# Layer-norm reciprocal square roots by Ln and Exp on ScalarE, and mixed-V stores on another queue

## The chip, the cores and the metric

The kernel runs on one core of a Trainium2 chip. The metric is the device time of one execution in microseconds (us), as a median over runs; the kernel before takes 297.19 us (three runs, 296.29 to 297.81). Engines are named as in the profile: PE is TensorE, PEld its weight loads, DVE VectorE, ACT ScalarE, POOL GpSimd, SP SyncE. A run is called slow when it lies over 1.5% above the fastest of the same kernel, the other runs fast.

## The reference, cut to what matters

Attention over blocks that a Sinkhorn-normalised matrix has mixed, then a Fourier mix of the result, a layer norm and a feed-forward network. The change is about the line with `sqrt`, and about how `v_sorted` reaches the attention.

```python
k_sorted = einsum('bhij,bhjcd->bhicd', P, k_b)     # P: five Sinkhorn steps on sort_net
v_sorted = einsum('bhij,bhjcd->bhicd', P, v_b)     # the "mixed V"
x   = softmax(scale * q_b @ k_sb.T) @ v_sb         # laid out (4, 768, 512)
u   = x + real(fft(fft(x, axis=1), axis=2))
un  = (u - mean(u)) / sqrt(var(u) + 1e-6)          # over 512 columns
out = u + relu(un @ w_ch1) @ w_ch2                 # 512 -> 2048 -> 512
```

## The kernel before

The kernel first collects all its operations with `P.add(costs, fn, r=reads, w=writes)` and then orders them with a small scheduler of its own. `costs` names the engines that may run the operation, each with (time that it occupies the engine, time to its result). The scheduler, where an operation may run on ACT or DVE, takes the engine that its plan says is free first. The hardware then runs each engine's operations in the planned order.

The layer norm of one group (three tiles of 128 rows; two groups in each of four batches, so eight norms) works on a 128x3 tile of variances, on GpSimd:

```python
P.add({"POOL": (0.25, 0.25)}, lambda _: G.tensor_scalar(
    mv.ap[:, :, 1], mv.ap[:, :, 1], 1e-6, None, op0=ALU.add), ...)
P.add({"POOL": (0.9, 0.9)}, lambda _: G.tensor_tensor(
    ny.ap, mv.ap[:, :, 1], mhalf, op=ALU.pow), ...)          # (var + eps) ** -0.5
P.add({"POOL": (0.2, 0.2)}, lambda _: G.tensor_tensor(
    nm.ap, mv.ap[:, :, 0], ny.ap, op=ALU.mult), ...)
P.add({"POOL": (0.25, 0.25)}, lambda _: G.tensor_scalar(
    nm.ap, nm.ap, -1.0, None, op0=ALU.mult), ...)
...  # then un = u * ny + nm, on ACT or DVE, three tiles
```

The mixed V of a pair of batches is stored to DRAM by SyncE and gathered back into another layout by GpSimd:

```python
for hb in range(2):                 # the pair's two batches
    for k_ in range(3):
        P.add({"SP": (0.4, 4.2)}, lambda _, ...:
              nc.sync.dma_start(vdr[t][w64, cols], vm[w64, cols]), ...)
        o = P.add({"POOL": (1.3, 1.3)}, lambda _, ...:
              nc.gpsimd.dma_start(vsb[...], vdr[t][w64, cols]...), ...)
```

The feed-forward's first matmul fills a PSUM bank with four matmuls; the bank is then emptied with a ReLU (`hr`) by ACT or DVE, as the plan decides. This emptying is called an eviction below.

The softmax here doesn't subtract the row's maximum and nothing guards it: scores larger than these inputs give would overflow.

Of the kernel before, what the change touches and what calls it, by code (L numbers as in the profile page):

```python
# [9 lines left out]
F32 = mybir.dt.float32  # L10
F16 = mybir.dt.float16
AF = mybir.ActivationFunctionType
ALU = mybir.AluOpType
# [8 lines left out]
DM = 512  # L22
# [348 lines left out]
def kernel(  # L371
# [10 lines left out]
    nc = tc.nc  # L382
# [6 lines left out]
    def ct(name, shape, dtype):  # L389
        return const.tile(shape, dtype, name=name)  # L390

    P = Plan()

    def many(name, n, shape, dtype):
        P.pool(name, [ct(f"{name}{i}", shape, dtype) for i in range(n)])
# [39 lines left out]
    many("y", 1, [128, 4, 2 * NK], F16)  # L435
    many("hi", 1, [128, 258], F16)
    many("u", 6, [128, DM], F32)
    many("un", 2, [128, DM], F16)
    many("ut", 2, [128, 4, GT], F16)
    tab = ct("tab", [128, 2, 2, 257], F32)  # L440
    cs = ct("cs", [128, 2, 3, 2 * NK], F16)
# [10 lines left out]
    vbn = ct("vbn", [128, D], F16)  # L452
    rows = ct("rows", [128, 3 * B], mybir.dt.uint32)
    negone = ct("negone", [128, 1], F32)
    mhalf = ct("mhalf", [128, 3], F32)
    mone = ct("mone", [128, 3], F32)
    many("rz", 4, [128, 6], F32)
    many("st", 3, [128, 6], F32)
    many("mv", 2, [128, 3, 2], F32)
# [66 lines left out]
    def hk(g):  # L526
        return [("h", g, fc) for fc in range(16)]

    def load_v(t, hf, prio):
        if t == 0:  # L530
            load(nat[0][:, 3072 * hf:3072 * hf + 3072].rearrange(
                "p (c d) -> p c d", d=D),
                vv[0:128, 48 * hf:48 * hf + 48, :], 1572864,
                [("nat", 0, hf)] + hk(0)[8 * hf:8 * hf + 8], prio)
            return
        keys = kqk(2 * hf) + kqk(2 * hf + 1)
        past = {o for n in keys for d_ in (P.wr, P.rd) for o in d_.get(n, ())}
        for n in keys:
            P.wr[n], P.rd[n] = [], []
        for r in range(3 * hf, 3 * hf + 3):  # L540
            load(nat[1][:, 1024 * r:1024 * r + 1024].rearrange(
                "p (c d) -> p c d", d=D),
                vv[128:256].rearrange(
                    "p (c r) d -> p r c d", r=6)[:, r], 690000,
                [("nat", 1, r)], prio + 0.01 * r, after=tuple(past))
            P.ops[-1].late = 0.0
            for n in keys:
                P.wr[n].append(P.ops[-1])
# [10 lines left out]
    V = nc.vector  # L559
    for n in range(NEB):  # L560
# [3 lines left out]
              tag="ebz")  # L564
    for n in range(2):
# [4 lines left out]
        vsb[0:96, :, D:D + 1], 1.0 / XSC), w=["vsz"], prio=-200.0, tag="vsz")  # L570
    P.add({"POOL": (0.1, 0.4)}, lambda _: nc.gpsimd.memset(
        pmt[:, 4:7, DM:DM + 2], 0.0), w=["pmz"], prio=-150.0, tag="small")
    for t_, val in ((negone, -1.0), (mhalf, -0.5), (mone, 1.0)):
        P.add({"POOL": (0.1, 0.4)}, lambda _, t_=t_, val=val:
              nc.gpsimd.memset(t_, val), w=["smalls"], prio=-199.0, tag="small")
    P.add({"POOL": (0.9, 0.9)}, lambda _: nc.gpsimd.tensor_tensor(
        mone, mone, mhalf, op=ALU.pow), r=["smalls"], w=["mone"], prio=-198.0,
        tag="small")

    early = dict(  # L580
        pw=(pw, sort_net.rearrange("b h i j -> (b h) i j"), 8192),
# [167 lines left out]
    def v_mix(t):  # L749
        bd = bdv16[t].rearrange("p g i -> p (g i)")  # L750
        stage = [i for n in range(4) for i in kqk(n)] if t else hk(0)
        vm = nat[1] if t else hr[1].rearrange("p a b -> p (a b)")
        vmk = [] if t else hk(1)
        n4 = nat[t].rearrange(
            "p (r c d) -> p r c d" if t else "p (c r d) -> p r c d",
            r=6, d=D)
        for n in range(12):
            r, hf = divmod(n, 2)
            ps = Buf("pm", "pf")

            def f(_, r=r, hf=hf, ps=ps):
                o = ps.ap.rearrange("p (c d) -> p c d", d=D)
                nc.tensor.matmul(o, bd, n4[:, r, 8 * hf:8 * hf + 8],
                                 start=True, stop=(t == 1))
                if t == 0:
                    nc.tensor.matmul(
                        o, bd, vbn[:, None, :].broadcast_to([128, 8, D]),
                        start=False, stop=True)
            P.add(pe(mm(512, 2 - t)), f,
                  r=[("nat", t, r if t else hf), ("bdv16", t)] + stage  # L770
                  + (["vbn"] if t == 0 else []), w=[ps], tag="vmix")
            P.add({"ACT": act(512), "DVE": dve(512)},
                  lambda e, n=n, ps=ps: copy(
                      e, vm[:, 512 * n:512 * n + 512], ps.ap),
                  r=[ps] + vmk, w=[("vm", t, n)] + (
                      [("nat", 1, r)] if t else []), tag="vev")
        for hb in range(2):
            w64 = slice(64 * hb, 64 * hb + 64)
            for k_ in range(3):
                cols = slice(2048 * k_, 2048 * k_ + 2048)  # L780
                P.add({"SP": (0.4, 4.2)}, lambda _, w64=w64, cols=cols:
                      nc.sync.dma_start(vdr[t][w64, cols], vm[w64, cols]),
                      r=[("vm", t, n) for n in range(4 * k_, 4 * k_ + 4)]
                      + (stage if t else vmk), w=[("vdr", t, k_, hb)],
                      prio=P.prio + 6 * hb, tag="vst")
                o = P.add({"POOL": (1.3, 1.3)},
                          lambda _, k_=k_, w64=w64, cols=cols:
                          nc.gpsimd.dma_start(  # L788
                              vsb[32 * k_:32 * k_ + 32, w64, 0:D],
                              vdr[t][w64, cols].rearrange(  # L790
                                  "g (c d) -> c g d", d=D)),
                          r=[("vdr", t, k_, hb), "vsz"],
                          w=[("vsb", k_, hb)],
                          prio=P.prio if hb == 0 or t else 38.0,
                          tag="vgt", nbytes=690000)
                gets[t, hb].append(o)
# [390 lines left out]
    def dft2(b, g):  # L1187
# [11 lines left out]
        for tt in range(3):  # L1199
# [62 lines left out]
                mv.ap[:, tt, :], st.ap), r=[st], w=[(mv, tt)], tag="bna")  # L1262
        ny, nm = Buf("ny"), Buf("nm")
        mvs = [(mv, tt) for tt in range(3)]
        G = nc.gpsimd
        P.add({"POOL": (0.25, 0.25)}, lambda _: G.tensor_scalar(  # L1266
            mv.ap[:, :, 1], mv.ap[:, :, 1], 1e-6, None, op0=ALU.add),
            r=mvs, w=[(mv, 3)], tag="ln")
        P.add({"POOL": (0.9, 0.9)}, lambda _: G.tensor_tensor(
            ny.ap, mv.ap[:, :, 1], mhalf, op=ALU.pow),  # L1270
            r=[(mv, 3), "mone"], w=[ny], tag="ln")
        P.add({"POOL": (0.2, 0.2)}, lambda _: G.tensor_tensor(
            nm.ap, mv.ap[:, :, 0], ny.ap, op=ALU.mult),
            r=[(mv, 3), ny], w=[nm], tag="ln")
        P.add({"POOL": (0.25, 0.25)}, lambda _: G.tensor_scalar(
            nm.ap, nm.ap, -1.0, None, op0=ALU.mult), r=[nm], w=[(nm, 1)],
            tag="ln")
        lns.append(P.ops[-1])
        ut = Buf("ut")
        uts[b, g] = ut  # L1280
        for tt in range(3):
            un, pt, u = Buf("un"), Buf("pf"), us[b, g][tt]

            def f(e, tt=tt, un=un, u=u):
                if e == "ACT":
                    nc.scalar.activation(un.ap, u.ap, AF.Identity,  # L1286
                                         scale=ny.ap[:, tt:tt + 1],
                                         bias=nm.ap[:, tt:tt + 1])
                else:
                    V.tensor_scalar(un.ap, u.ap, ny.ap[:, tt:tt + 1],  # L1290
                                    nm.ap[:, tt:tt + 1],
                                    op0=ALU.mult, op1=ALU.add)
            P.add({"ACT": (0.72, 0.81), "DVE": (0.45, 0.55)}, f,
                  r=[u, ny, (nm, 1)], w=[un], tag="un")
            if b > 0:
                P.add({"SP": (1.3, 4.0)}, lambda _, tt=tt, un=un:
                      nc.sync.dma_start_transpose(
                          ut.ap[:, :, 128 * tt:128 * tt + 128], un.ap),
                      r=[un], w=[(ut, tt, 1)], tag="uX")
                continue  # L1300

            def f(_, un=un, pt=pt):
                p16 = pt.ap.bitcast(F16)
                for c in range(4):
                    nc.tensor.matmul(
                        p16[:, 128 * c:128 * c + 128],
                        un.ap[:, 128 * c:128 * c + 128], idh,
                        is_transpose=True)
            P.add(pe(0.27), f, r=[un, "pack"], w=[pt, (ut, tt)], tag="uT")
            P.add({"ACT": act(512), "DVE": dve(512, 2.0)},  # L1310
                  lambda e, tt=tt, pt=pt: copy(
                      e, ut.ap[:, :, 128 * tt:128 * tt + 128],
                      pt.ap.bitcast(F16)[:, 0:512].rearrange(
                          "p (c s) -> p c s", c=4)),
                  r=[pt], w=[(ut, tt, 1)], tag="utev")
# [156 lines left out]
```

## Time and profile before

| profiled run of before | value |
|---|---|
| span | 293.2 us |
| PE busy | 257.1 us (88%) |
| ACT busy | 145.1 us (49%) |
| DVE, POOL busy | 173.9 us, 84.8 us |
| mean granted PE clock (share of the full clock) | 0.963 |
| ACT table loads | 1 |

The forty slices and the stretches say where PE has holes: before 143 us it has some, after that none. The timelines of ACT, DVE and PE say which bank waits for which eviction. A bracket such as `[2.56 <-ACT ex L1030]` at the end of a line means that the engine stood still 2.56 us before this instruction, and that the named write by ACT ended the wait. The lines themselves stand in the prediction.

### The profile page before, as it was taken

To read this page: it belongs to the slowest core of one execution; us is meant where nothing else is said; L and a number is where in the kernel's file an instruction comes from. 1 tells how busy PE (TensorE), PEld (TensorE's weight loads), DVE (VectorE), ACT (ScalarE), POOL (GpSimd) and SP (SyncE) were. 2 spreads that over 40 slices of the span, in tenths; PEclk is the share of its full clock that TensorE was granted. 3 is DMA by queue.
4 is the path that set the end of the run, shared out by engine and by line. 5 is a ranking of instruction groups with operands and counts; after the bars stand their busy time and mean duration, and the time that the engine had idled before them with its cause. 6 is when DMAs were issued, how large, how long until landed. Compare 5 with 4: busy or idle time off the path is not lost.

```text
span 293.2 us, 5526 instructions
## 1 busy us (share of the span) xinstructions
PE 257.1 (88%) x2124; PEld 146.9 (50%) x2124; DVE 173.9 (59%) x407; ACT 145.1 (49%) x307; POOL 84.8 (29%) x120
## 2 busy tenths in 40 slices
PE   0698697769999999696999999999999999999980
PEld 0255484465555464453557456456555545545530
DVE  6899879896999997384999452146124315310020
ACT  2289649666642586643697126327514505605400
POOL 8914843049730056830220001023000212200021
PEclk9999759987999999999999999999999999999997
DMA  7999999999996369999303011411311131141001
GB/s 128 202 203 287 217 229 173 213 209 141 164 173 122 80 162 221 170 144 153 92 22 57 2 72 36 56 72 50 56 72 37 36 56 72 36 92 36 0 36 72
DMA packets 56543, 32.60 MB, mean 111 GB/s; under 512 B 42842, under 2 KB 51560, under 8 KB 56516
## 3 DMA queue, kind: packets, MB, share of 16 engines
q0 software_dynamic: 36592, 21.46, 50.6%
q1 hardware_dynamic: 19926, 10.80, 16.8%
q8 instruction: 16, 0.26, 0.4%
q14 instruction: 9, 0.07, 0.1%
HBM read 32.12 MB, written 9.44 MB: 142 GB/s over the span
## 4 chain that ended last, share of the span: by engine, by line
PE 47%; DMA 3%; issue 1%; DVE 1%; POOLq 0%; DVEq 0%
PE bank L1326 21%; PE bank L1347 20%; DMA out_dram<-u,rows 3%; PE bank L1221 1%; PE bank L1133 1%; PE bank L1060 1%; PE bank L1225 1%; PE bank L1021 1%; POOLq L1467 0%; PE bank L966 0%; PE bank L1138 0%; PE bank L1209 0%; DVE u L1355 0%; DVE u L1245 0%; PE bank L1143 0%
## 5 line engine op out<-in xcount | busy, mean ns | idle before, releaser
L1326 PE MATMUL bank<-ut,w1sb 128*128 128x384 f16 x512 | 93.8, 330 | 3.0 <-DVE u L1355 2.8
L1338 ACT ACTIVATE hr<-bank 128x384 f16<-128x384 f32 x109 | 53.3, 490 | 71.1 <-PE bank L1326 70.4
L1347 PE MATMUL bank<-w2sb,hr 128*128 128x512 f16 x384 | 87.8, 379 | 0.0
L1326 PEld LDWEIGHTS <-w1sb 128*128 128x128 f16 x512 | 48.9, 99 | 38.0 <-issue 5.0
L1347 PEld LDWEIGHTS <-hr 128*128 128x128 f16 x384 | 36.9, 98 | 41.7 <-issue 0.2
L1355 DVE TENSOR_TENSOR u<-bank,u 128x512 f32<-128x512 f32 x24 | 16.5, 690 | 54.5 <-PE bank L1347 54.2
L1030 ACT ACTIVATE ex<-bank 96x384 f32<-96x384 f32 x64 | 28.4, 485 | 10.7 <-PE bank L1021 10.2
L1368 POOL DMA_INDIRECT out_dram<-u,rows x12 | 12.1, 1006 | 72.4 <-DVE u L1355 54.4
L1266 POOL TENSOR_SCALAR mv<-mv 128x3 f32<-128x3 f32 x8 | 1.9, 240 | 78.8 <-DVE mv L1261 75.7
L788 POOL DMA_DIRECT2D vsf<-vdr x12 | 13.0, 1088 | 34.8 <-DMA vdr<-kq 23.4
L1060 PE MATMUL bank<-vsf,eb 97*128 97x65 f16 x416 | 18.6, 206 | 2.6 <-DMA vsf<-vdr 1.6
L1060 PEld LDWEIGHTS <-eb 97*128 97x128 f16 x416 | 16.8, 107 | 5.2 <-issue 2.8
L1045 ACT ACTIVATE eb<-ex,negone 96x384 f16<-96x384 f32 x31 | 18.5, 613 | 0.3
L486 POOL DMA_DIRECT2D kq<-in_q_dram x20 | 16.4, 833 | 6.9 <-DMA kq<-in_k_dram 2.1
L1286 ACT ACTIVATE un<-u,nm,ny 128x512 f16<-128x512 f32 x15 | 12.2, 811 | 11.4 <-DMA ut<-un 9.1
L1076 DVE TENSOR_TENSOR rt<-bank,rz 128x384 f16<-128x384 f32 x32 | 17.2, 549 | 0.4
L1245 DVE SCALAR_TENSOR_TENSOR u<-rt,bank 128x510 f32<-128x510 f16 x12 | 8.1, 679 | 15.5 <-DMA out_dram<-u,rows 9.9
L1233 DVE SCALAR_TENSOR_TENSOR u<-rt,bank 128x512 f32<-128x512 f16 x12 | 8.0, 685 | 14.8 <-PE bank L1225 14.8
L1259 DVE BATCH_NORM_STATS2 st<-u 128x6 f32<-128x512 f32 x24 | 16.1, 682 | 0.2
L1021 PE MATMUL bank<-qt,ks 64*128 64x96 f16 x256 | 12.8, 213 | 3.7 <-ACT ex L1030 2.9
L966 PE MATMUL bank<-bdk,kq 128*64 128x128 f16 x192 | 10.6, 228 | 3.4 <-ACT ex L1030 1.5
L694 ACT CAST ks<-bank 128x384 f16<-128x384 f32 x18 | 8.2, 484 | 10.7 <-PE bank L966 10.6
(137 smaller groups left out, 317.3 us busy)
## 6 DMA issues: line engine op xcount, KB each, us to landing
kq<-in_k_dram POOLq DMA_DIRECT2D x8, 384.0 KB, 10.1
vsf<-vdr POOLq DMA_DIRECT2D x12, 256.0 KB, 6.9
w1sb<-in_moe_w_ch_dram POOLq DMA_DIRECT2D x4, 512.0 KB, 16.9
w2sb<-in_moe_w_ch_dram POOLq DMA_DIRECT2D x4, 512.0 KB, 19.3
out_dram<-u SPq DMA_DIRECT2D x8, 256.0 KB, 2.0
hr<-in_v_dram POOLq DMA_DIRECT2D x2, 768.0 KB, 9.4
kq<-in_q_dram POOLq DMA_DIRECT2D x4, 384.0 KB, 13.9
vdr<-hr SPq DMA_DIRECT2D x6, 256.0 KB, 5.0
```

Of the source, the lines that this page charges most:

```text
L486: o = P.add({eng: c}, lambda _: e.dma_start(dst, src), r=r, w=w, prio=prio, nbytes=nbytes, tag="load", after=after, behind=gate)
L788: nc.gpsimd.dma_start(vsb[32 * k_:32 * k_ + 32, w64, 0:D], vdr[t][w64, cols].rearrange("g (c d) -> c g d", d=D)),
L1021: nc.tensor.matmul(pss[h2].ap[:, BLK * j:BLK * j + BLK], ks.ap[rows, 4 * g + j, :], qt.ap[rows, c0:c0 + BLK])
L1030: nc.scalar.activation(ex.ap, pss[h2].ap[0:96, 0:384], AF.Exp, scale=SCALE),
L1045: nc.scalar.activation(ed, src, AF.Identity, bias=negone[0:96])
L1060: nc.tensor.matmul(po.ap[:, 65 * T:65 * T + 65], eb.ap[:, e0:e0 + 128], vsf[:, vi:vi + 65], start=(n == 0), stop=(n == len(WIN[T]) - 1), s ...
L1076: P.add({"DVE": (0.45, 0.56)}, lambda _: V.tensor_tensor(rt.ap[:, :, D * h:D * h + D], po3()[:, :, 0:D], rz.ap[:, :, None].broadcast_to([1 ...
L1259: P.add({"DVE": (0.6, 0.69)}, lambda _, u=u, st=st: V.bn_stats(st.ap, u.ap), r=[u], w=[st], tag="bn")
L1326: nc.tensor.matmul(ps.ap[:, 0:GT], w1sb[:, c, 128 * fc:128 * fc + 128], ut.ap[:, c, :], start=(c == 0), stop=(c == 3))
L1338: nc.scalar.activation(hr[g][:, fc, :], ps.ap[:, 0:GT], AF.Relu)
L1347: nc.tensor.matmul(ps.ap, hr[g][:, fc, 128 * tt:128 * tt + 128], w2sb[:, fc, :], start=(fc == 0), stop=(fc == 15))
L1355: V.tensor_tensor(u.ap, ps.ap, u.ap, op=ALU.add),
```

## The change

The intent: take the pow and its three helpers off GpSimd, where a norm took 1.84 us, and make the reciprocal root as exp(-0.5 ln(var + eps)) on ScalarE, with one vector operation for -mean times that. Where DVE normalises a tile, it now computes (u - mean) * ny (left out of the diff below). A first dummy Ln is to fetch the function tables of ScalarE early; an ACT_TABLE_LOAD in a profile is the fetching of one set of them. Beside it, a third `un` buffer, and the mixed-V stores re-ordered: pair 1's are issued by GpSimd, those of batch 1 stand behind batch 0's gather. The line with `late` adds 1.2 us to a planned landing time; it is no instruction.

```diff
-    many("un", 2, [128, DM], F16)
+    many("un", 3, [128, DM], F16)
 ...
+            P.ops[-1].late = 1.2                      # first V load, plan only
 ...
+    P.add({"ACT": (1.5, 1.6)}, lambda _: nc.scalar.activation(
+        mone, eps, AF.Ln), r=["eps"], w=["mone"], prio=-9000.0, tag="small")
 ...
-                P.add({"SP": (0.4, 4.2)}, lambda _, ...: nc.sync.dma_start(...)
+                P.add({"POOL": (0.7, 4.5)} if t else {"SP": (0.4, 4.2)}, ...
+                      behind=() if t or hb == 0 else gets[0, 0][-1:],
 ...
-        (four GpSimd operations: add eps, pow, mult, mult by -1)
+        P.add({"ACT": (0.17, 0.24)}, lambda _: nc.scalar.activation(
+            ny.ap, mv.ap[:, :, 1], AF.Ln, bias=eps), ...)
+        P.add({"ACT": (0.17, 0.24)}, lambda _: nc.scalar.activation(
+            ny.ap, ny.ap, AF.Exp, scale=-0.5), ...)
+        P.add({"DVE": (0.08, 0.18)}, lambda _: V.scalar_tensor_tensor(
+            nm.ap, mv.ap[:, :, 0], -1.0, ny.ap, op0=ALU.mult, op1=ALU.mult), ...)
```

More of the change, by code (lines that the diff above doesn't have):

```diff
@@ L454 @@
     negone = ct("negone", [128, 1], F32)
-    mhalf = ct("mhalf", [128, 3], F32)
-    mone = ct("mone", [128, 3], F32)
+    eps = ct("eps", [128, 1], F32)
+    mone = ct("mone", [128, 1], F32)
     many("rz", 4, [128, 6], F32)
@@ L572 @@
         pmt[:, 4:7, DM:DM + 2], 0.0), w=["pmz"], prio=-150.0, tag="small")
-    for t_, val in ((negone, -1.0), (mhalf, -0.5), (mone, 1.0)):
-        P.add({"POOL": (0.1, 0.4)}, lambda _, t_=t_, val=val:
-              nc.gpsimd.memset(t_, val), w=["smalls"], prio=-199.0, tag="small")
-    P.add({"POOL": (0.9, 0.9)}, lambda _: nc.gpsimd.tensor_tensor(
-        mone, mone, mhalf, op=ALU.pow), r=["smalls"], w=["mone"], prio=-198.0,
-        tag="small")
+    P.add({"DVE": (0.06, 0.12)}, lambda _: V.memset(eps, 1e-6), w=["eps"],
+          prio=-9100.0, tag="small")
+    P.add({"POOL": (0.1, 0.4)}, lambda _: nc.gpsimd.memset(negone, -1.0),
+          w=["smalls"], prio=-199.0, tag="small")
+    P.add({"ACT": (1.5, 1.6)}, lambda _: nc.scalar.activation(
+        mone, eps, AF.Ln), r=["eps"], w=["mone"], prio=-9000.0, tag="small")
     early = dict(
@@ L780, in v_mix @@
                 cols = slice(2048 * k_, 2048 * k_ + 2048)
-                P.add({"SP": (0.4, 4.2)}, lambda _, w64=w64, cols=cols:
-                      nc.sync.dma_start(vdr[t][w64, cols], vm[w64, cols]),
+                P.add({"POOL": (0.7, 4.5)} if t else {"SP": (0.4, 4.2)},
+                      lambda e, w64=w64, cols=cols:
+                      (nc.gpsimd if e == "POOL" else nc.sync).dma_start(
+                          vdr[t][w64, cols], vm[w64, cols]),
+                      behind=() if t or hb == 0 else gets[0, 0][-1:],
                       r=[("vm", t, n) for n in range(4 * k_, 4 * k_ + 4)]
@@ L1264, in dft2 @@
         mvs = [(mv, tt) for tt in range(3)]
-        G = nc.gpsimd
-        P.add({"POOL": (0.25, 0.25)}, lambda _: G.tensor_scalar(
-            mv.ap[:, :, 1], mv.ap[:, :, 1], 1e-6, None, op0=ALU.add),
-            r=mvs, w=[(mv, 3)], tag="ln")
-        P.add({"POOL": (0.9, 0.9)}, lambda _: G.tensor_tensor(
-            ny.ap, mv.ap[:, :, 1], mhalf, op=ALU.pow),
-            r=[(mv, 3), "mone"], w=[ny], tag="ln")
-        P.add({"POOL": (0.2, 0.2)}, lambda _: G.tensor_tensor(
-            nm.ap, mv.ap[:, :, 0], ny.ap, op=ALU.mult),
-            r=[(mv, 3), ny], w=[nm], tag="ln")
-        P.add({"POOL": (0.25, 0.25)}, lambda _: G.tensor_scalar(
-            nm.ap, nm.ap, -1.0, None, op0=ALU.mult), r=[nm], w=[(nm, 1)],
-            tag="ln")
+        P.add({"ACT": (0.17, 0.24)}, lambda _: nc.scalar.activation(
+            ny.ap, mv.ap[:, :, 1], AF.Ln, bias=eps), r=mvs + ["eps"],
+            w=[(ny, 0)], tag="ln")
+        P.add({"ACT": (0.17, 0.24)}, lambda _: nc.scalar.activation(
+            ny.ap, ny.ap, AF.Exp, scale=-0.5), r=[(ny, 0)], w=[ny], tag="ln")
+        P.add({"DVE": (0.08, 0.18)}, lambda _: V.scalar_tensor_tensor(
+            nm.ap, mv.ap[:, :, 0], -1.0, ny.ap, op0=ALU.mult, op1=ALU.mult),
+            r=mvs + [ny], w=[nm], tag="ln")
         lns.append(P.ops[-1])
@@ L1289, in f @@
                 else:
-                    V.tensor_scalar(un.ap, u.ap, ny.ap[:, tt:tt + 1],
-                                    nm.ap[:, tt:tt + 1],
-                                    op0=ALU.mult, op1=ALU.add)
+                    V.tensor_scalar(un.ap, u.ap, mv.ap[:, tt, 0:1],
+                                    ny.ap[:, tt:tt + 1],
+                                    op0=ALU.subtract, op1=ALU.mult)
             P.add({"ACT": (0.72, 0.81), "DVE": (0.45, 0.55)}, f,
-                  r=[u, ny, (nm, 1)], w=[un], tag="un")
+                  r=[u, ny, nm] + mvs, w=[un], tag="un")
             if b > 0:
```

## The prediction

> **What bounds the kernel now.** I first read the page's forty slices, then a table of three stretches, then the chain that ended last.
>
> ```profile
> PE   0698697769999999696999999999999999999980
> ACT  2289649666642586643697126327514505605400
> 0.00:143.00 143.00, 115.37 (x1199) 69.84 (x1199) 117.17 (x279) 82.53 (x178) 66.71 (x90) 0.94 1.18 176
> 143.00:281.00 138.00, 137.84 (x909) 75.45 (x909) 54.93 (x127) 62.53 (x130) 15.10 (x27) 1.00 0.20 49
> PE 47%; DMA 3%; issue 1%; DVE 1%; POOLq 0%; DVEq 0%
> ```
>
> The columns of the stretches are length, then busy time of PE, PEld, DVE, ACT and POOL, then PE clock, DMA share and GB/s. The span is 293.2 us. From 143 us to 281 us TensorE is busy 137.84 of 138.00 us, and the chain is PE followed by PE. There, time is added only by something that makes PE wait. Before 143 us PE has 27.6 us of holes; any gain must come out of those. ScalarE is 58% busy before 143 us and 45% after, so it is not the bound, but it empties the PSUM banks that PE fills.
>
> The layer norm as it stands, in the timeline of GpSimd, and the one table load in the groups:
>
> ```profile
> L626 ACT ACT_TABLE_LOAD x1 | 1.3, 1283 | 0.7 <-PEq L1456 0.7
> 59.38 0.25 POOL L1266 TENSOR_SCALAR mv<-mv 128x3 f32<-128x3 f32 x1 [8.82 <-DVE mv L1261]
> 59.71 0.89 POOL L1269 TENSOR_TENSOR ny<-mv,mhalf 128x3 f32<-128x3 f32 x1
> 60.68 0.19 POOL L1272 TENSOR_TENSOR nm<-mv,ny 128x3 f32<-128x3 f32 x1
> 60.96 0.26 POOL L1275 TENSOR_SCALAR nm<-nm 128x3 f32<-128x3 f32 x1
> ```
>
> One layer norm (there are eight) takes 61.22 - 59.38 = 1.84 us on an otherwise idle engine. A late one, in the timelines of PE, ACT and DVE:
>
> ```profile
> 179.78 4.71 PE L1326 MATMUL bank<-ut,w1sb 128*128 128x384 f16 x28
> 181.28 0.49 ACT L1338 ACTIVATE hr<-bank 128x384 f16<-128x384 f32 x1 [0.16 <-PE bank L1326]
> 181.93 0.49 ACT L1338 ACTIVATE hr<-bank 128x384 f16<-128x384 f32 x1 [0.16 <-PE bank L1326]
> 182.58 0.49 ACT L1338 ACTIVATE hr<-bank 128x384 f16<-128x384 f32 x1 [0.16 <-PE bank L1326]
> 183.54 0.55 DVE L1290 TENSOR_SCALAR un<-u,ny,nm 128x512 f16<-128x512 f32 x1 [1.92 <-POOL nm L1275]
> ```
>
> PE fills a bank every 0.65 us (four matmuls), and ACT empties each in 0.49 us just after. While GpSimd computes the norm, these evictions run on. And the largest hole that the change could close, on ACT and on PE:
>
> ```profile
> 118.35 0.81 ACT L1286 ACTIVATE un<-u,nm,ny 128x512 f16<-128x512 f32 x1 [3.69 <-DMA ut<-un]
> 119.59 0.20 PE L1021 MATMUL bank<-qt,ks 64*128 64x96 f16 x1 [2.56 <-ACT ex L1030]
> ```
>
> ACT waits 3.69 us because the third normalised tile needs one of two un buffers back from a DMA transpose; the exponentials queue behind it and PE stands for 2.56 us.
>
> **What the Trainium skill says.** (1) "ScalarE: Activation LUTs", section "Table sets: the hidden batching unit": functions are loaded in named sets; natural_log_exp_and_others has both exp and ln and would need one load. That is the author's hope: a dummy Ln at the start is to bring in a set that serves both. (2) "ScalarE activation tables: per-element evaluation and per-set limits", section "What a function is on this engine": functions in different sets are one load of 1283 ns apart. The trace agrees on the size: its one load took 1283 ns. (3) "ScalarE: Activation LUTs", section "What ACT_TABLE_LOAD costs", adds a drain of about 1380 ns, 2.66 us in all. The trace can't decide this: the load ended at 2.00 us and the next activation began at 2.95 us, released by DVE, which bounds a tail at 0.95 us but says nothing of a load in a busy stream. (4) "TensorE: Matmul & The Clock Gate", section "Part 1: The HAM clock gate": idle windows of about 3.4 us bring half clock. [...] the granted clock was 0.64 in 30 to 40 us and 0.68 in 60 to 70 us, where PE has holes.
>
> **The change part by part.**
>
> *Table loads.* The instruction order of the changed kernel settles the main point. It has 18 table loads on ScalarE where there was one. Every Ln is preceded by a load of one set and every Exp by a load of another; the set chosen for Ln is never kept for Exp. The hoped-for single load did not come about. So 17 x 1.283 = 21.8 us are added to ACT; with 16 small activations of about 0.22 us (a 128x4 copy takes 0.21 us, the 32x64 exp 0.255 us) 3.5 us more: 25 us, taking ACT from 145 to about 170 us. GpSimd loses eight chains of 1.84 us, about 13 us busy, worth nothing in itself.
>
> *Late norms.* Block per norm on ACT: 1.28 + 0.2 + 1.28 + 0.25 = 3.0 us. Take the norm at 181.6 us. The new order keeps 28 matmuls (seven banks) on PE, and on ACT: two evictions, load, Ln, load, Exp, eviction. The second eviction ends at 181.77; load to 183.05, Ln to 183.25, load to 184.6, Exp to 184.85. Three banks rotate: the bank that ended at 182.54 and was emptied at 183.07 is now emptied at 185.34, while PE wants it at 183.84: a hole of 1.5 us. The next evictions on both ACT and DVE stand behind the normalisation of un, which waits for Exp: about 0.6 us more. So 2.1 us a norm. Five norms lie there (about 150, 182, 204, 229 and 251 us), four in runs of the first feed-forward matmul and one in the attention stretch with ACT 84% busy: 5 x 2.1 = 10.5 us, all on the path.
>
> *Early norms.* Batch 0: PE waits for the transposed tiles. Without the loads the chain would take some 0.7 us, against 1.84; with them ACT (busy until 59.9) runs load, Ln, an eviction, load, Exp to about 63.5, against 61.2. About 2 us for the first group, and the second pair of loads stands among the copies of the first group's transposes, so 2 us again: +4 us. Batch 1's first group, at 108 us, blocks evictions and exponentials on a busy ACT: +2 us.
>
> *Start.* The dummy Ln waits for a DVE memset behind two others, about 2.6 us; a second load then ends at about 4.2 us, where the first Exp of the Sinkhorn chain began at 2.95 us: +1.25 us at the head of a serial chain.
>
> *V stores and gathers.* Pair 0: the stores of batch 0 now go first, all three before those of batch 1; the third was the fifth of six in a burst of 4.97 us. Its gather can leave 1.5 us earlier, and PE waited 1.59 us for it at 34.92: -1.5 us. Pair 1: the queue of SyncE loses a burst of 8.37 us, so transposes of un start earlier. But now a gather on GpSimd's queue blocks the stores behind it until its own store has landed (4.5 us before). Three such rounds of about 5 to 6 us: the last gather of batch 2 lands near 123 us, against 118; PE wanted it at 122.6 and will be later itself. Near zero, with a risk of some us.
>
> *Third un buffer.* Takes away the 3.69 us wait: -2.5 us.
>
> Sum: +10.5 + 4 + 2 + 1.25 - 1.5 - 2.5 = +13.75 us. I take 2 us back for slack in the early holes that I can't follow: about +12 us on 297.2, so 309 us.
>
> **The rivals.** (a) *ACT has room.* With 45% busy late, the loads might hide behind the second feed-forward matmul, whose 0.22 us matmuls need no eviction for long. For: one norm in six or so may slip there, and the early gains are real. Against: the order puts the Ln inside the seven-bank runs. Then the result is 297 to 302 us. (b) *Drain at each load.* If each switch costs 2.66 us, another 16 x 1.38 = 22 us land on ACT, most of it on PE: 320 to 327 us. The program has no separate drain beside the loads, which speaks against it. (c) *The gather becomes the wait.* If the stores in GpSimd's queue hold back the values of batch 2, PE waits at about 123 us for 3 to 6 us, and half clock follows: 312 to 316 us. (d) *Gains win.* Early holes of 27.6 us close by more than the loads add: under 294 us. The layer norm's new chain is longer, not shorter, so I give it little.
>
> **Range and chances.** The count of loads and their 1283 ns are certain; how much of a 3 us block reaches PE is not. If half of it does, 302; if a drain comes too, above 320. I give 300 to 322 us 8 in 10. Slower by over 2% begins at 303.1 us: 0.80. Within 2%: 0.16. Faster by over 2%: 0.04.
>
> **What would show it.** The changed profile should have 18 table loads of 1283 ns; ACT busy near 170 us; after each late Exp a PE wait of 1.5 to 2.5 us on bank L1325 for an ACT eviction; PE no longer gapless after 150 us, with a lack of some 10 us; the first Sinkhorn Exp near 4.2 us; no 3.69 us wait of un on the transpose. Load to next activation over 1 us would mean rival (b); a PE wait on vsf above 2 us, rival (c). If the late PE stretch stays gapless, my main step is wrong.

## The result, and the profile after

The kernel after took 310.56 us (median of four runs, 308.2 to 311.69) against 297.09 us for the kernel before (four runs). The ratio is 1.0444, 95% interval 1.0371 to 1.0517: slower. Ratios here are the mean time of one kernel's fast runs over that of the other's of the same rounds, so they are not quite the ratio of the quoted medians.

The same views of the kernel after: two rows of the forty slices, the two stretches (the second now ends at 297 us), and the chain that ended last.

```profile
PE   0798898849998998996979997999899799799990
ACT  4376758879731899341995048027614705805500
0.00:143.00 143.00, 117.46 (x1177) 71.78 (x1178) 114.71 (x280) 90.91 (x186) 63.76 (x81) 0.89 1.18 174
143.00:297.00 154.00, 144.64 (x929) 77.22 (x927) 61.38 (x144) 72.67 (x145) 7.14 (x8) 0.98 0.17 45
PE 40%; ACT 6%; DMA 4%; DVE 3%; issue 2%; POOLq 0%; DVEq 0%
```

PE was busy 137.84 of 138.00 us late in the kernel before; now it is busy 144.64 of 154.00 us. The late stretch has 9 us of holes, and the chain, which was PE and nearly nothing else, now contains ACT with 6%. ACT's busy time is 163.6 us instead of 145.1. And the same 2124 matmuls keep PE busy for 266.7 us instead of 257.1, at a mean granted clock of 0.933 instead of 0.963: besides the holes there are slow matmuls.

One late boundary of the kernel after, in the timelines of ACT and PE (start, duration, engine, line, operation):

```profile
188.06 0.49 ACT L1337 ACTIVATE hr<-bank 128x384 f16<-128x384 f32 x1 [0.16 <-PE bank L1325]
188.57 1.28 ACT L1269 ACT_TABLE_LOAD   x1
189.87 0.30 ACT L1269 ACTIVATE ny<-mv,eps 128x3 f32<-128x3 f32 x1
190.18 1.28 ACT L1272 ACT_TABLE_LOAD   x1
191.47 0.20 ACT L1272 ACTIVATE ny<-ny 128x3 f32<-128x3 f32 x1
191.58 0.47 ACT L1337 ACTIVATE hr<-bank 128x384 f16<-128x384 f32 x1
192.11 0.81 PE L1325 MATMUL bank<-ut,w1sb 128*128 128x384 f16 x4 [1.48 <-ACT hr L1337]
193.31 10.48 PE L1346 MATMUL bank<-w2sb,hr 128*128 128x512 f16 x40 [0.39 <-DVE hr L1334]
```

From 188.57 to 191.58 us ACT empties no bank, 3.0 us long. PE uses up its free banks and stands 1.48 us, until the eviction that was queued behind the Exp. Then it stands 0.39 us more. An Ln that did 0.30 us of work cost a load of 1.28 us each way. The same pattern comes back at 219.51 us (1.12 and 0.34, the first one ended by an eviction on DVE), at 245.04 (1.48 and 0.39) and at 269.08 (1.48 and 0.39).

### The profile page after: what moved, and what is told of

Same layout as the page of the kernel before. It is cut to its first block, busy times and chain, and to the rows that moved or that the text cites. A ratio compares the mean times of both kernels' runs of the same rounds, so it can differ in the third digit from the quotient of the medians.

```text
span 309.7 us, 5507 instructions
## 1 busy us (share of the span) xinstructions
PE 266.7 (86%) x2124; PEld 150.9 (49%) x2124; DVE 178.2 (58%) x426; ACT 163.6 (53%) x331; POOL 73.8 (24%) x91
## 4 chain that ended last, share of the span: by engine, by line
PE 40%; ACT 6%; DMA 4%; DVE 3%; issue 2%; POOLq 0%; DVEq 0%
PE bank L1346 20%; PE bank L1325 16%; DMA out_dram<-u,rows 4%; ACT L1269 2%; PE bank L1225 1%; DVE un L1289 1%; ACT L1272 1%; PE bank L1064 1%; ACT y L1155 1%; PE bank L1229 1%; ACT hr L1337 1%; DVE hr L1334 1%; PE bank L1137 1%; PE bank L1025 1%; ACT ny L1269 0%
## 5 line engine op out<-in xcount | busy, mean ns | idle before, releaser
L1325 PE MATMUL bank<-ut,w1sb 128*128 128x384 f16 x512 | 95.3, 331 | 8.5 <-ACT hr L1337 4.4
L1337 ACT ACTIVATE hr<-bank 128x384 f16<-128x384 f32 x106 | 51.1, 489 | 84.8 <-PE bank L1325 84.3
L1346 PE MATMUL bank<-w2sb,hr 128*128 128x512 f16 x384 | 90.7, 387 | 1.5 <-DVE hr L1334 1.2
L1346 PEld LDWEIGHTS <-hr 128*128 128x128 f16 x384 | 37.6, 99 | 45.3 <-issue 5.7
L1367 POOL DMA_INDIRECT out_dram<-u,rows x12 | 11.6, 968 | 161.6 <-DVE u L1354 146.0
L1034 ACT ACTIVATE ex<-bank 96x384 f32<-96x384 f32 x64 | 28.2, 482 | 12.0 <-PE bank L1025 10.5
L1064 PE MATMUL bank<-vsf,eb 97*128 97x65 f16 x416 | 19.4, 208 | 3.3 <-DVE u L1258 1.6
L1064 PEld LDWEIGHTS <-eb 97*128 97x128 f16 x416 | 17.5, 107 | 6.2 <-issue 3.9
L719 PE MATMUL bank<-hr,pack 128*128 128x512 f16 x12 | 5.4, 623 | 9.9 <-DMA hr<-in_v_dram 9.9
L1025 PEld LDWEIGHTS <-ks 64*128 64x128 f16 x256 | 7.8, 102 | 10.6 <-issue 8.9
L1334 DVE TENSOR_SCALAR hr<-bank 128x384 f16<-128x384 f32 x22 | 12.1, 552 | 1.4 <-PE bank L1325 1.1
## 6 DMA issues: line engine op xcount, KB each, us to landing
kq<-in_k_dram POOLq DMA_DIRECT2D x8, 384.0 KB, 12.2
```

Source lines behind the costliest of these rows:

```text
L1025: nc.tensor.matmul(pss[h2].ap[:, BLK * j:BLK * j + BLK], ks.ap[rows, 4 * g + j, :], qt.ap[rows, c0:c0 + BLK])
L1034: nc.scalar.activation(ex.ap, pss[h2].ap[0:96, 0:384], AF.Exp, scale=SCALE),
L1064: nc.tensor.matmul(po.ap[:, 65 * T:65 * T + 65], eb.ap[:, e0:e0 + 128], vsf[:, vi:vi + 65], start=(n == 0), stop=(n == len(WIN[T]) - 1), s ...
L1325: nc.tensor.matmul(ps.ap[:, 0:GT], w1sb[:, c, 128 * fc:128 * fc + 128], ut.ap[:, c, :], start=(c == 0), stop=(c == 3))
L1334: V.tensor_scalar(hr[g][:, fc, :], ps.ap[:, 0:GT], 0.0, None, op0=ALU.max)
L1337: nc.scalar.activation(hr[g][:, fc, :], ps.ap[:, 0:GT], AF.Relu)
```

## The experiments

Theory A: the 17 added table loads are the cause, because evictions queue behind them on ACT. Rival B: the new order of work, the moved stores and the longer chain of the norm are. The kernels below tell them apart. Positions of matmuls, where quoted, are the starts of the same matmul, counted by its line, in two profiles.

### One load in place of 18

```diff
+    nc.scalar.preload_act_table_set("natural_log_exp_and_others")
     P.add({"ACT": (1.5, 1.6)}, lambda _: nc.scalar.activation(
         mone, eps, AF.Ln), r=["eps"], w=["mone"], prio=-9000.0, tag="small")
```

With a set loaded that serves both functions, the build adds no other load. The built program has one load instead of 18, and on every engine the order of all other instructions is that of the kernel after (of the 2124 matmuls in the two traces none has changed its place). This is as clean as a test can be.

> The kernel after, with one load of a table set that serves both Ln and Exp placed by hand ahead of the first activation; the 17 other loads are gone and nothing else moves (the order of instructions on every engine is that of the kernel after). Theory A (the table loads are the cause): late PE holes of 1.5 and 0.4 us at the four group boundaries and the waits of 0.4 to 1.5 us in the first norms shrink below 0.3 us each, the granted clock of 143 us to the end goes back to 0.99 or more, and the time falls to 294 to 298 us, level with the kernel before; ScalarE's busy time falls by 17 x 1.28 = 21.8 us to about 142. Rival B (the new order of work, the moved stores and the longer chain from variance to normalised row through ScalarE are what costs): the time stays at 304 us or more, and the holes at the boundaries stay over 1 us.

Measured: 296.09 us (295.56 to 298.0), ratio to before 0.9996, interval 0.9919 to 1.0074; the output is correct. ACT's busy time is 142.2 us. The same boundary in its ACT and PE timelines, and below it a late stretch:

```profile
182.74 0.29 ACT L1270 ACTIVATE ny<-mv,eps 128x3 f32<-128x3 f32 x1
183.06 0.20 ACT L1273 ACTIVATE ny<-ny 128x3 f32<-128x3 f32 x1
183.66 0.49 ACT L1338 ACTIVATE hr<-bank 128x384 f16<-128x384 f32 x1 [0.39 <-PE bank L1326]
180.86 4.71 PE L1326 MATMUL bank<-ut,w1sb 128*128 128x384 f16 x28
143.00:281.00 138.00, 138.00 (x917) 75.40 (x917) 59.46 (x139) 60.14 (x134) 6.21 (x7) 1.00 0.19 49
```

PE runs its 28 matmuls without a wait, and ACT waits for PE, not the other way round. The loads alone are worth 310.56 - 296.09 = 14.5 us, in other words the whole loss. Rival B's 304 us or more did not come. From 143 to 281 us PE is gapless again, at the full clock. One detail of the expectation missed: in the first norms not all waits shrank below 0.3 us. PE still waits 0.97 and 0.67 us for the transposes at 63.69 and 64.95 us, much as in the kernel before (1.06 and 0.67).

### The loads alone, in the kernel before

```diff
+        P.add({"ACT": (0.0, 0.0)}, lambda _: (
+            nc.scalar.preload_act_table_set("natural_log"),
+            nc.scalar.preload_act_table_set("exp_and_others")),
+            r=mvs, w=["loads"], tag="ld")
         G = nc.gpsimd                       # the norm stays on GpSimd
```

With a planned cost of zero the order on all engines stays that of the kernel before.

> The kernel before, with two table loads (Ln's set, then Exp's) put into ScalarE's queue at each of the eight norms, behind the variances, and nothing else: the norm stays on GpSimd and the order on every engine is unchanged. Theory A: 16 x 1.28 us = 20.5 us of ScalarE time at the same places bring most of the loss: 308 to 313 us (estimate 310). Rival B: under 301 us, since neither the order nor the chain of the norm changes.

Measured: 311.97 us (310.35 to 312.62), ratio 1.0504, interval 1.0423 to 1.0584. Its ACT and PE timelines, at a boundary:

```profile
191.97 1.28 ACT L1266 ACT_TABLE_LOAD   x1
193.26 1.28 ACT L1267 ACT_TABLE_LOAD   x1
195.10 1.46 PE L1330 MATMUL bank<-ut,w1sb 128*128 128x384 f16 x8 [1.72 <-ACT hr L1342]
```

No Ln, no Exp, no norm that depends on the loads, and the loss is there in full. The loads hurt as time that ACT doesn't empty banks; that the norm also waits for them is not needed.

### Twice as many

```diff
+            nc.scalar.preload_act_table_set("exp_and_others"),   # useless, ahead of each Ln
             nc.scalar.activation(ny.ap, mv.ap[:, :, 1], AF.Ln, bias=eps)
 ...
+            nc.scalar.preload_act_table_set("natural_log"),      # useless, ahead of each Exp
             nc.scalar.activation(ny.ap, ny.ap, AF.Exp, scale=-0.5)
```

> The kernel after with one useless load ahead of each of the 16 needed ones at the norms (34 loads in all), same order everywhere. It measures what a load costs where it stands. Theory A: another 16 x 1.28 = 20.5 us of ScalarE time, at the late norms fully in PE's way, in the early ones in part: 324 to 333 us. Rival B (loads mostly hidden, the order costs): under 317 us.

Measured: 337.6 us (335.72 to 338.88), ratio 1.1372. That is 27 us above the kernel after, more than the 16 x 1.283 = 20.5 us of ACT time that was put in, and above my range. First a late boundary, from its PE timeline, then one late stretch of it and one of the kernel after, each with 131 matmuls (PE clock is the third number from the end).

```profile
204.13 0.81 PE L1329 MATMUL bank<-ut,w1sb 128*128 128x384 f16 x4 [4.06 <-ACT hr L1341]
234.00:264.00 30.00, 26.24 (x131) 13.51 (x131) 7.48 (x15) 13.99 (x26) 0.00 (x0) 0.90 0.14 40
```

```profile
219.00:245.00 26.00, 23.70 (x131) 12.80 (x131) 8.24 (x17) 12.09 (x25) 0.00 (x0) 1.00 0.16 46
```

The hole went from 1.48 to 4.06 us: 2.58 us, as long as two more loads (2 x 1.283 = 2.57 us). Once the free banks are used up, every further load is paid in full. On top of that the granted clock fell from 1.00 to 0.90 in such a stretch, and the same number of matmuls took 26.24 instead of 23.70 us: 2.5 us more in slow matmuls, behind the hole of 3.12 us that ended at 234.11 us (1.12 us in the kernel after). Over the whole kernel PE is busy 274.6 us instead of 266.7 for the same matmuls. That is enough for the excess over 20.5 us.

### The same 18 loads, but the plan knows them

```diff
-        P.add({"ACT": (0.17, 0.24)}, lambda _: nc.scalar.activation(
+        P.add({"ACT": (1.58, 1.65)}, lambda _: nc.scalar.activation(
             ny.ap, mv.ap[:, :, 1], AF.Ln, bias=eps), ...
-        P.add({"ACT": (0.17, 0.24)}, lambda _: nc.scalar.activation(
+        P.add({"ACT": (1.48, 1.55)}, lambda _: nc.scalar.activation(
             ny.ap, ny.ap, AF.Exp, scale=-0.5), ...
```

> The kernel after, with the plan told 1.58 us for the Ln and 1.48 us for the Exp in place of 0.17 us each; 18 loads remain. If the loss came from a plan that did not know the loads, the scheduler gives part of it back by putting more evictions on VectorE around them: 302 to 307 us. If the loads hurt because ScalarE's queue runs in order and the evictions of the next product stand behind them whatever the plan says: 308 to 312 us. I expect the second with 60 per cent.

Measured: 294.35 us (292.97 to 297.01), ratio to before 0.9903, interval 0.983 to 0.9977. I had given 60 per cent to 308 to 312 us, and even my hopeful case was 302. This was the largest surprise: all 18 loads are in the trace, and the loss is gone. The boundary in its ACT, DVE and PE timelines:

```profile
181.34 1.28 ACT L1269 ACT_TABLE_LOAD   x1
182.63 0.30 ACT L1269 ACTIVATE ny<-mv,eps 128x3 f32<-128x3 f32 x1
182.83 0.47 ACT L1337 ACTIVATE hr<-bank 128x384 f16<-128x384 f32 x1
183.32 1.28 ACT L1272 ACT_TABLE_LOAD   x1
181.48 1.21 DVE L1334 TENSOR_SCALAR hr<-bank 128x384 f16<-128x384 f32 x2 [0.32 <-PE bank L1325]
183.43 1.21 DVE L1334 TENSOR_SCALAR hr<-bank 128x384 f16<-128x384 f32 x2 [0.74 <-PE bank L1325]
179.33 4.71 PE L1325 MATMUL bank<-ut,w1sb 128*128 128x384 f16 x28
```

ACT does its loads at the same place. But an eviction now runs between the two, and while each load lasts, DVE takes two evictions; in the kernel after it took one and then stood 2.44 us for the Exp. PE's 28 matmuls run without a wait. Over the whole kernel DVE empties 40 of these banks instead of 22. So "a load costs 3 us of ACT" was right, and "therefore the banks wait" was a property of the plan, which believed 0.17 us. This run moved the order everywhere, not only at the boundaries, so not all of the gain comes from these. By the starts of the last matmuls, the planned kernel is 5.3 us ahead of the kernel after at the last attention product with V (160.47 against 165.73 us) and 16.9 us ahead at the last second-layer matmul (284.33 against 301.18). So 11.6 us fall in the stretch with the four boundaries (in part because it holds 674 matmuls there instead of 686), and these are clean.

### The other parts of the change, one by one

These are in the kernel before, with the norm on GpSimd: the stores and the buffer together; the buffer alone; the stores with the plan's 1.2 us; the stores alone. Each is a part of the diff above.

> The kernel before with the rest of the change: third un buffer, pair 1's mixed-V stores on GpSimd, those of batch 1 behind the gather of batch 0; the norm stays on GpSimd with its pow. Theory A: 293 to 297 us, since these parts save about 2.5 us of the un wait at 120 us and up to 1.5 us of the gather and cost nothing. Rival B (moved stores or order cost): 302 us or more.

Measured: 299.24 us, ratio 1.0072, interval 0.9983 to 1.0161. A miss for both theories: I expected a gain or at least 302 us, and it is level.

> The kernel before with a third un buffer and nothing else of the change; the schedule is made anew, so the order of work moves too. Asked because the stores and the third buffer together gave 1.0072 where a gain was expected. Theory C (the moved stores cost it): this one is level or a little faster, 294 to 297 us, with the 2.5 us hole near 120 us gone. Theory D (the third buffer lets the scheduler pick an order that is worse later): 298 to 300 us, with one hole of 4 us or more before batch 1's first projection near 141 us, as in the run with both parts.

Measured: 296.63 us, ratio 0.9995, interval 0.9927 to 1.0063. The third buffer does what it should and is worth nothing. The hole of 2.56 us near 120 us is gone, and the 125th first-layer matmul of the feed-forward starts 3.7 us earlier (116.57 against 120.22 us). But in its PE timeline the next wait has grown:

```profile
138.56 1.44 PE L1326 MATMUL bank<-ut,w1sb 128*128 128x384 f16 x4 [4.09 <-DVE u L1355]
```

In the kernel before this hole was 2.51 us, at 139.54. DVE waits there for a row buffer `u` whose scatter to the output has not landed (5.78 us in its timeline, 4.20 us in the kernel before). The matmuls behind it are slow as well: the four in the line take 1.44 us, in the kernel before 0.81, and the granted clock from 137 to 147 us is 0.83 against 1.00. The 137th first-layer matmul, at 141.47 us, is already 0.4 us later than in the kernel before. The hole over 4 us is what theory D had named; its loss of time did not come.

> The kernel before with the moved mixed-V stores alone (pair 1's on GpSimd, batch 1's behind the gather of batch 0). Theory C (the stores cost what the run with both parts lost): 298 to 300 us. Theory D (the third buffer's order costs it): 294.5 to 297 us; the first product with V starts within 1 us of the kernel before.

Measured: 301.59 us, ratio 1.0177, interval 1.0126 to 1.0228, a little over the range of theory C.

> The kernel before with the moved mixed-V stores, but without the 1.2 us that the changed kernel's plan adds to the landing time of the first V load (that one changes no instruction, only the planned order). Theory E (the stores on GpSimd push back what stands behind them in its queue, the Q and K loads of the next pair and the scatter of the rows of u, so that VectorE waits longer for a u buffer near 135 us): still 298 to 302 us, with the scatter before that wait issued 2 us or more later than in the kernel before. Rival F (the order planned with the 1.2 us is what cost it): 294.5 to 297.5 us.

Measured: 300.02 us, ratio 1.0106, interval 1.0054 to 1.0158. The moved stores cost 1 to 2%, with or without the plan's 1.2 us. The scatter in GpSimd's timeline and the wait in DVE's, of the kernel before and then of the one with the stores alone:

```profile
129.70 1.10 POOL L1368 DMA_INDIRECT out_dram<-u,rows  x1 [0.31 <-DVE rz L1073]
137.27 0.69 DVE L1245 SCALAR_TENSOR_TENSOR u<-rt,bank 128x510 f32<-128x510 f16 x1 [4.20 <-DMA out_dram<-u,rows]
```

```profile
133.28 1.09 POOL L1371 DMA_INDIRECT out_dram<-u,rows  x1 [0.72 <-DMA kq<-in_q_dram]
139.38 0.69 DVE L1248 SCALAR_TENSOR_TENSOR u<-rt,bank 128x510 f32<-128x510 f16 x1 [6.87 <-DMA out_dram<-u,rows]
140.59 0.53 PE L969 MATMUL bank<-bdk,kq 128*64 128x128 f16 x6 [5.57 <-DVE rt L1079]
```

GpSimd issues its queue in order: six stores more, each behind the copy that it stores, then the gathers, the Q and K loads and the scatter. The scatter leaves 3.6 us later, DVE waits 6.87 us for the buffer instead of 4.20, and an eviction behind it holds PE for 5.57 us. Theory E fits in both numbers. But the order of work moves as well, and in the kernel with one load, which has the same stores, the scatter leaves at 129.56 us; so the cost is shown for this order, not for every one.

### With one load: is there something better?

Four variants of the one-load kernel, each against before: two `un` buffers again; the stores as before; the stores as before without the plan's 1.2 us; and the stores as before with seven `u` buffers, which fit only with smaller pools elsewhere.

> The kernel with one table load for all, with two un buffers as before; the stores stay moved. Theory: the un wait of 2.5 us near 120 us comes back, 297 to 299 us. If the buffer is worth nothing: 295 to 296.5 us, and the two kernels differ only by which order the scheduler happened on.

Measured: 297.25 us, ratio 1.0038, interval 0.9982 to 1.0094. The time is inconclusive: inside the noise of the three-buffer kernel. The theory's wait did not come back: from 105 to 132 us PE has no hole above 0.16 us. This order has another one, of 4.83 us, that ends at 137.83 us.

> The kernel with one table load for all, with the mixed-V stores as they were before (all on SyncE, batches alternating); third un buffer kept. If the stores' move is worth 1 us or more either way it shows as 295 us or 297 us against the 296.1 us of the kernel with one load; my expectation is within 1 us of it.

Measured: 295.45 us, ratio 0.9926, interval 0.9856 to 0.9997.

> The kernel with one table load and the stores as before, without the 1.2 us in the plan for the first V load: that is, the layer norms by Ln and Exp with a single table load and a third un buffer, and nothing else of the change. Expected level with the kernel with the 1.2 us: 293.5 to 296.5 us. If the 1.2 us in the plan is worth something: 296.5 us or more.

Measured: 294.97 us (293.31 to 295.8), ratio 0.9907, interval 0.986 to 0.9954. As expected. The norm by Ln and Exp with a single load, the third buffer and nothing else is about 1% faster than the kernel before. So is the planned kernel above; for both this is less than the 2% that counts as faster. The order of work also differs from the kernel before on every engine, so it isn't shown that the norm, and not the order, brings the 1%. The two together were not run.

> The kernel with one table load and the stores as before, with seven u buffers for six (to fit, two un buffers, three rz and two st buffers, and the dummy first Ln dropped). If the 2.5 to 3.5 us hole near 139 us, which stands in every kernel so far, comes from VectorE waiting for the scatter of an old u buffer, it falls below 1.5 us and the time to 292 to 295 us. If another wait takes its place (or the smaller pools bring their own): 295 to 298 us.

Measured: 297.63 us, ratio 1.0012. The other branch came true: DVE still waits, and PE has other waits.

```profile
142.24 0.69 DVE L1244 SCALAR_TENSOR_TENSOR u<-rt,bank 128x510 f32<-128x510 f16 x1 [5.01 <-DMA out_dram<-u,rows]
143.44 0.60 PE L1220 MATMUL bank<-vcx,y 128*128 128x256 f16 x4 [2.16 <-DVE rt L1075]
```

Its scatter left at 135.49 us, 5.8 us later than in the kernel before, so a seventh buffer met a later landing. With three pools made smaller at once, this doesn't settle what a seventh buffer would be worth. That stays open.

## Why the prediction was right or wrong

The text said 309 us and slower with 0.80; the time was 310.56 us. By its steps:

- **Table loads: right.** 18 loads of 1.28 us are in the trace, and taking away 17 takes away the whole loss. ACT's busy time rose to 163.6, not to about 170 us, mainly because in the new order ACT normalises 9 tiles instead of 15 (7.2 us instead of 12.2).
- **Late norms: right, the price somewhat low.** The kernel after and the one-load kernel differ by the loads alone, so the starts of the same matmul show what the loads cost. From the 145th first-layer matmul (147.65 us in the kernel after) to the last second-layer matmul (301.18 us) the kernel after falls back from 3.0 to 15.7 us: 12.8 us, where the step said 10.5. Two boundaries cost 2.2 us each and one 1.8, against the predicted 2.1. The norm in the attention stretch cost 2.7, with holes of 1.21 and 0.75 us at 157.55 and 159.44 us that the one-load kernel lacks. The boundary at 192 us cost 3.9, since slow matmuls came behind its hole, a term that the sum lacked here: the 40 second-layer matmuls at 193.31 us took 10.48 us, against 8.79 us for as many elsewhere.
- **Early norms: near at first, then half of it was gone.** The step said 4 + 2 us. By the same comparison the first matmul of the feed-forward is 3.3 us later from the loads, and the 113th, at 119.68 us, 5.8 us. But at 147.65 us only 3.0 are left: the one-load kernel loses time just before, with a wait of 3.41 us at 138.35 us and a granted clock of 0.50 from 137 to 143.7 us.
- **Start: the delay was real, its price was not.** The first Exp of the Sinkhorn chain began at 4.17 us instead of 2.95. But the first matmul that mixes V began at 17.1 us in both kernels, so the 1.25 us were hidden.
- **V stores and gathers: wrong.** "Its gather can leave 1.5 us earlier [...] -1.5 us" failed: the wait of PE on the gathered V at 34.92 us did go, but the product with V began at 36.3 us, later. With the stores alone that wait was even longer, 2.55 us, and the product began at 36.03 us. For pair 1, "near zero, with a risk of some us" under-rated the risk. The stores alone cost 1 to 2% in the kernel before. I had looked for a gather that comes late, as in rival (c); what came late was the scatter behind it in the same queue.
- **Third un buffer: right in place, wrong in the sum.** The 3.69 us wait vanished, but "-2.5 us" was taken back at the next wait, for the `u` buffer.
- **The rivals.** (b), the drain, fell: the activation starts 0.01 us after its load (190.18 + 1.28 = 191.46, Exp at 191.47 us). (c) did not show: the kernel after has no such wait of PE on the gathered V. (a), "ACT has room", I had rejected because "the order puts the Ln inside the seven-bank runs". For this program that was correct. As a statement on the work it was not: with the true costs in the plan the Ln stays inside such a run and PE does not wait.
- **One reading of a page was wrong.** Point (4) set the page's idle windows of about 3.4 us beside stretches where the longest wait of PE was 1.59 us (30 to 40 us) and 1.06 us (60 to 70 us). They show half clock near holes, but not that length.

The sum by parts: the loads were put at 10.5 + 4 + 2 us less 2 us of slack, 14.5 us, and that is what they measured (310.56 - 296.09). The total is in part luck: by the starts above, the late part was put too low and the early part too high. The rest was put at 1.25 - 1.5 - 2.5 = -2.75 us, and came to nothing: the one-load kernel, which has all but the delay at the start, stands at 0.9996 of the kernel before. Whether that is why the kernel came out 1.6 us above 309 can't be told, since its runs spread from 308.2 to 311.69 us. The step that carried the verdict, the loads in the way of the evictions, is shown by the one-load kernel and by the loads alone in the kernel before.

## What to carry to other kernels

Count the table loads in the built program before believing that an activation is small: an Ln next to Exps cost 1.28 us to get there and 1.28 us back, unless a set that serves both is loaded by hand first. If such a cost must stay, tell the scheduler: the same 18 loads cost some 14 us in a plan that took each pair of load and function for 0.17 us, and in a plan that knew them the kernel was 1% under the kernel before. And when a wait has been removed, look at once for the next wait on the same chain; here a gain of 3.7 us at 117 us was gone at 141 us.

## What the Trainium skill lacked or had wrong

- "ScalarE: Activation LUTs", section "What ACT_TABLE_LOAD costs": the 1283 ns of a load agree (1283 ns for each group of loads), but the drain of about 1380 ns, 2.66 us per switch, is not seen. In a busy stream the load began 0.02 us after the eviction before it (188.57 us) and the next activation 0.01 us after the load, and 16 added loads lengthened a boundary's hole by 2.58 us for two of them.
- The same page, section "Table sets: the hidden batching unit", counts one load for ln followed by exp. Here that held only once the shared set was loaded by hand: this build gave each Ln and each Exp a load of its own, 18 in all. With natural_log_exp_and_others loaded first there was one, and 14.5 us went.
- "ScalarE activation tables: per-element evaluation and per-set limits", section "Table sets in the compiler and the runtime", says that loads are placed per block, greedily for the longest run. In this build the set loaded for an Ln was never kept for the Exp behind it, though one set serves both: 18 loads. Whether a block ended between the two is not on record.
- No page that I read says that the cost of a load on ScalarE depends on whether other engines can empty the PSUM banks meanwhile: 18 loads at 310.56 us, the same 18 at 294.35 us.
- "TensorE: Matmul & The Clock Gate", section "Part 1: The HAM clock gate", puts half clock after an idle window of about 3.4 us (the page tells elsewhere of shorter idles with that effect, without a length). Here shorter waits were enough: 1.48 and 0.39 us at one of four boundaries (a granted clock of 0.94 in 191 to 219 us), but not at the other three, and not a wait of 2.51 us at 139.54 in the kernel before (1.00 in 137 to 147 us). What decides between them is open.
